# Full 128x128 tiles in place of four 128x32 column tiles, in stretches of TensorE work that hold no attention product

## The chip, the cores and the metric

The kernel runs on one core of one Trainium2 chip. The metric is the device time of one execution in microseconds. Before the change three runs gave 878.08, 880.55 and 883.79 us; the median is 880.55 us.

## The reference, cut to what matters

Two layers of one program, each an attention part A and an MLP part B, on 2048 tokens of width 576 in bf16:

```python
def _A_ref(x, wqkv, wo):          # 32 heads of 18, sliding window of 256, causal
    qkv = (x @ wqkv) ...
    scores = einsum("bhqd,bhkd->bhqk", q, k) * 18 ** -0.5
    p = softmax(where(mask, scores, -1e9))
    o = einsum("bhqk,bhkd->bhqd", p, v)
    return o.reshape(B, S, D) @ wo

def _B_ref(x, w1, b1, w2, b2):    # F = 4608
    h = gelu(layernorm(x) @ w1 + b1)
    return h @ w2 + b2

x = x + A(layernorm(x)); x = x + B(layernorm(x))   # both of these twice
```

The products with `w2` (the second MLP product) and with `wo` (the output product) are those that the change is about.

## The kernel before

Each layer is cut into four chunks of four token tiles (128 tokens each), eight chunks in all. For a chunk the kernel makes Q, K and V, the scores of eight groups of four heads, the exponentials, the product of the probabilities with V, the output product, layer norm, and the MLP in three parts of 12 blocks of 128 hidden columns. Work of neighbouring chunks is woven together, so that the exponentials of one chunk on ScalarE run while TensorE does the MLP of another.

Nothing of this order is written out by hand. Every step is a `Task` given to `Plan.add`, with its engine, its reads and writes, a cost and a priority. `Plan.schedule` simulates the engines and emits the tasks in the order of their simulated starts; a table of small nudges shifts priorities by stage. A task on TensorE has a `mode`, the tile shape in which it runs, and the planner adds `SWITCH` = 0.095 to the cost of a task whose mode differs from that of the task before:

- `"f"`: full 128x128 tiles. The QKV projection of chunk 0 (`two_out`, line 782), transposes, and the filler products (line 669).
- `"h"`: two tiles of 64 rows. The first MLP product (`G_part`, line 1058) and QKV of later chunks (line 822).
- `"r"`: four tiles of 32 rows, one for each head of a group. The scores (`scores`, line 891).
- `"c"`: four tiles of 32 columns. The product of probabilities with V (`pv`, line 938), which needs them since each head has only 20 columns, and all that goes through the helper `quad` (line 768): the second MLP product (`mm2`), the output product (`tail`, by `two_out`), and QKV of chunk 1 (also `two_out`).

`quad` computes what one full tile could: 128 rows, 128 output rows in PSUM, 288 moving columns. It issues four products of the same moving operand, each with 32 of the 128 stationary columns, into the four 32-partition parts of one bank. In this shape it can stand beside `pv` with no change of mode between them.

Each bank that a second MLP product fills collects 12 such quads, in two tasks of 6; one of the output product collects 5. VectorE then adds the bank to the residual (`resid`, lines 1001 to 1008). Scores are followed by exponentials on ScalarE (line 900) and the mask on GpSimd (line 921). Weights are loaded on SP's queue.

Of the kernel before, what the change touches and what calls it, by code (L numbers as in the profile page):

```python
# [158 lines left out]

class Task:  # L160
    __slots__ = ("idx", "eng", "fn", "reads", "writes", "cost", "lat", "prio", "dma", "ring", "handles", "alloc", "move", "desc",
                 "npred", "succ", "ready", "end", "plain", "fifo", "hold", "stage", "mode", "own", "port")

    def __init__(self, **kw):
        for k, v in kw.items():
# [21 lines left out]
class Plan:  # L187
# [18 lines left out]
        self.nudge = {}  # L206
        self.fifo_last = {}

    def add(self, eng, fn, reads=(), writes=(), dma=None, ring=4, cost=0.1, lat=0.1, prio=0.0, alloc=(), fifo=None, plain=False, after=(), move=0.0, desc=0, hold=False, mode="f", own=False, port=None):
        if eng == "dve" and fifo is None:  # L210
            fifo = self.chain
        stage = self.stage + self.part + ("+" if dma in ("w1", "w2", "xr") else "")
        prio += self.nudge.get(stage, 0.0)
        t = Task(idx=len(self.tasks), eng=eng, fn=fn, reads=tuple(reads), writes=tuple(writes), cost=cost, lat=lat, prio=prio,
                 dma=dma, ring=ring, alloc=tuple(alloc), handles=tuple({r for r in tuple(reads) + tuple(writes) if isinstance(r, Bank)}),
                 plain=plain, move=move, desc=desc, fifo=fifo, hold=hold, stage=stage, mode=mode, own=own,
                 port=(eng == "pool" and dma is None) if port is None else port)
        pred = set()
        for r in t.reads:
            if r in self.lw:  # L220
                pred.add(self.lw[r])
        for w in t.writes:
            pred.update(self.rd.get(w, ()))
            if w in self.lw:
                pred.add(self.lw[w])
        for w in after:
            pred.update(self.rd.get(w, ()))
        for w in t.writes:
            self.lw[w] = t
            self.rd[w] = []  # L230
        for r in t.reads:
            self.rd.setdefault(r, []).append(t)
        order = set()
        if fifo is not None:
            if fifo in self.fifo_last:
                order.add(self.fifo_last[fifo])
            self.fifo_last[fifo] = t
        order -= pred
        for p in pred:
            p.succ.append((t, True))  # L240
        for p in order:
            p.succ.append((t, False))
        t.npred = len(pred) + len(order)
        for h in t.handles:
            h.left += 1
        self.tasks.append(t)
        return t

    def keep_warm(self, a, b, bank_free, extra):

        if self.warm_fn is None or a < self.warm_from:
            a = max(a, self.warm_from)
        n = int((b - a - 0.1) * 0.8 / 0.115)
        banks = [x for x in (7, 6, 5, 4) if bank_free.get(x, 1e9) <= a]
        if n < 1 or not banks:
            return
        h = Bank(())
        h.no = banks[0]
        t = Task(idx=-1, eng="pe", fn=lambda e: self.warm_fn(e, h.no, n), reads=("warm",), writes=(h,), cost=n * 0.115, lat=0.1, prio=0.0,
                 dma=None, ring=4, alloc=(), handles=(), plain=False, move=0.0, desc=0, fifo=None, hold=False, stage="", mode="f", own=False, port=False)  # L260
        extra.append((a, t))

    def schedule(self):
        free = {e: BEGIN for e in ENGS}
        mode = "f"
        port = 0.0
# [49 lines left out]
        order = []  # L316
# [4 lines left out]
        while len(order) < n:  # L321
            best = None
            cands = []
            for e in ENGS:
                for t in released[e]:
                    st = max(free[e], t.ready)
                    if t.port:
                        st = max(st, port)
                    got = ()
                    if t.alloc:  # L330
# [3 lines left out]
                        st = max(st, when)  # L334
# [23 lines left out]
            if t.port:  # L358
                port = st + t.cost
# [5 lines left out]
            if t.dma is not None:  # L365
# [3 lines left out]
                while over > 0 and q:  # L369
                    a, b, d = q[0]  # L370
# [33 lines left out]
            order.append((st, t))  # L404
        order = sorted(order + extra, key=lambda x: x[0])
        self.order = order
        for st, t in order:
            names = lambda rs: [n for r in rs for n in ([f"pb{b}" for b in r.banks()] if isinstance(r, Bank) else [r])]
            if t.plain:
                self.S.plain(t.eng, t.fn)  # L410
            else:
                self.S.add(t.eng, t.fn, names(t.reads), names(t.writes), dma=t.dma, ring=t.ring, own=t.own)
# [11 lines left out]
def build_kernel(nc, A_x, A_wqkv, A_wo, B_x, B_w1, B_b1, B_w2, B_b2, out):  # L424
# [7 lines left out]
    KD = 5  # L432
    NF = F // P
    NPT = 3
    NFH = NF // NPT
# [3 lines left out]
    HB = 288  # L439
# [23 lines left out]
    add = PL.add  # L463
# [127 lines left out]
    def mm_cost(n):  # L591
        return max(n / 2400.0, 0.026) + (0.003 if n > 64 else 0.0)
# [69 lines left out]
    for i in OUT:  # L662
        b = Bank((i,))
# [89 lines left out]
    def w2_of(k, hf):  # L753
        return (w2_x, "w2x") if k == NK - 1 and hf == NPT - 1 else (w2_sb, "w2s")
# [7 lines left out]
                desc=128 * WB, prio=prio)  # L762


    def quad(e, b, lhs, rhs, start, stop):
        ins = None
        for j in range(4):
            ins = e.matmul(bank(b)[32 * j:32 * j + 32, 0:HB], lhs[:, 32 * j:32 * j + 32], rhs, start=start, stop=stop,  # L768
                           tile_position=(0, 32 * j), skip_group_check=True)
        return ins  # L770

    def two_out(lhs, rhs, reads, prio, after=(), fill=FILL, mode="f"):

        bs = [Bank(fill), Bank(fill)]
        for o in range(2):
            def fn(e, o=o):
                ins = None
                for c in range(KD):
                    if mode == "c":
                        ins = quad(e, bs[o], lhs(c), rhs(c, o * HB), c == 0, c == KD - 1)  # L780
                    else:
                        ins = e.matmul(bank(bs[o])[:, 0:HB], lhs(c), rhs(c, o * HB), start=(c == 0), stop=(c == KD - 1))  # L782
                return ins
            add("pe", fn, reads=reads, writes=[bs[o]], cost=mm_cost(HB) * KD, lat=0.22, prio=prio, alloc=[bs[o]], after=after, mode=mode)
        return bs

    def heads_of(b):
# [240 lines left out]
    def h_of(k, hf, fl):  # L1028
        if k == NK - 1 and hf == 1:
            return hP[:, fl, :], f"hp{fl}"  # L1030
        return hT[:, fl, :], f"h{fl}"
# [49 lines left out]
    def mm2(k, hf, prio):  # L1081
        l, t0, nt = CH[k]
        wt, wn = w2_of(k, hf)
        for i in range(nt):
            t = t0 + i
            fin = hf == NPT - 1 and l == NL - 1
            PL.part = f".{i}"
            osl, wait = None, []
            if fin and t >= 4:
                osl, odst, ord_ = f"x{t}", x_out[:, t - 4, :], [f"yo{t}h0", f"yo{t}h1"]  # L1090
            elif fin:
                sn = xn_ctr[0] % NXN
                xn_ctr[0] += 1
                osl, odst, ord_ = f"n{sn}", xn[:, sn, 0:D], [f"xn{sn}", f"xd{sn}"]
                wait = ord_
            for hh in range(2):
                b = Bank(FILL if k < NK - 1 else FILL + (3, 2, 1, 0))
                for f0 in range(0, NFH, 6):
                    def fn(e, hh=hh, b=b, f0=f0, i=i):
                        ins = None  # L1100
                        for fl in range(f0, f0 + 6):
                            ins = quad(e, b, h_of(k, hf, fl)[0][:, i * 128:(i + 1) * 128], wt[:, fl, hh * HB:(hh + 1) * HB],
                                       fl == 0, fl == NFH - 1)
                        return ins
                    add("pe", fn, reads=[h_of(k, hf, fl)[1] for fl in range(f0, f0 + 6 if f0 or i + hh == 0 or k == NK - 1 and i < 2 else NFH)] + [f"{wn}{f0 // WB}"], writes=[b],
                        cost=6 * mm_cost(HB), lat=0.22, prio=prio + 0.05 * i, alloc=((b,) if f0 == 0 else ()), mode="c",
                        after=(wait if f0 == 0 else ()))
                resid(t, hh, b, prio, outp=osl)
            if fin:
                dma("sp", out_dram[t * P:(t + 1) * P, :], odst, reads=ord_, cls="o", ring=4, cost=0.5,  # L1110
                    prio=prio)
            elif hf == NPT - 1:
                ln_stats(t, prio)
        PL.part = ""
# [28 lines left out]
    for i in range(n0):  # L1143
# [36 lines left out]
    for k in range(NK + 1):  # L1180
        b = 4 * k
# [114 lines left out]
```

## Time and profile before

| | |
|---|---|
| median of three runs | 880.55 us (878.08 to 883.79) |
| the profiled execution | 880.96 us, span 879.3 us |
| granted TensorE clock, mean | 0.994 |
| TensorE products (PE) | busy 856.9 us, 97% of the span, 17901 products |
| TensorE weight loads (PEld) | busy 543.0 us, 62% |
| ScalarE (ACT) | busy 594.7 us, 68% |
| VectorE (DVE) | busy 394.1 us, 45% |
| GpSimd (POOL) | busy 378.0 us, 43% |
| DMA | 120.58 MB, mean 137 GB/s |

How to read it: a row of the groups names a source line, an engine, an operation, the tile written and the tile read, the tile shape on the array as rows*columns (128*32 is a column tile, 128*128 a full one), the shapes, and a count; then busy time in us and mean duration in ns; then the idle time of the engine just before and what ended it. Busy time counts overlapping products once, so busy time by count is not the duration of one. A row of the timeline has start and length in us, the engine, the line, and how many instructions were merged. A row of the chain has start, length and what the chain went through.

### The profile page before, as it was taken

The numbers are of one execution on the slowest core, as the hardware profiler recorded it, in microseconds if no ns is written. First come the engines' busy times: TensorE is split into PE (matmuls) and PEld (weight loads), VectorE is DVE, ScalarE is ACT, GpSimd is POOL, SyncE is SP. The second block draws the span as 40 slices with busy tenths as digits, with TensorE's granted clock in tenths as the row PEclk, the third lists the DMA queues.
The fourth block names the chain that finished last, engine by engine and source line by source line (L and its number), as shares of the span: only waits on it lengthen the run. The fifth ranks groups of instructions, "written<-read, shape, count | busy, mean of one in ns | idle before, by whom it ended". The sixth has DMA issues, their size and how long they took to land.

```text
span 879.3 us, 39623 instructions
## 1 busy us (share of the span) xinstructions
PE 856.9 (97%) x17901; PEld 543.0 (62%) x17901; DVE 394.1 (45%) x934; ACT 594.7 (68%) x741; POOL 378.0 (43%) x560
## 2 busy tenths in 40 slices
PE   9888999999999999999999999999999899999998
PEld 7545556556566566565665665756656556557667
DVE  5877433555246442383434732654323353234012
ACT  4985797778667787564874887648687579771730
POOL 3875564385145662264431853426444176222100
PEclk9998999999999999999999999999999999999999
DMA  6799524471576722986367444675337963446320
GB/s 181 154 180 197 121 87 126 149 165 54 163 156 130 178 101 90 194 111 154 107 147 196 102 128 135 102 191 135 117 124 167 216 145 98 145 149 156 123 84 31
DMA packets 181913, 120.58 MB, mean 137 GB/s; under 512 B 107441, under 2 KB 181745, under 8 KB 181745
## 3 DMA queue, kind: packets, MB, share of 16 engines
q1 hardware_dynamic: 181744, 118.05, 55.1%
q8 instruction: 141, 2.31, 1.0%
q14 instruction: 28, 0.22, 0.1%
HBM read 90.10 MB, written 2.36 MB: 105 GB/s over the span
## 4 chain that ended last, share of the span: by engine, by line
PE 90%; DMA 5%; DVE 2%; issue 1%; ACT 1%; POOL 1%; SPq 0%; DVEq 0%; POOLq 0%
PE ps L768 36%; PE ps L1058 32%; PE ps L822 9%; PE ps L891 6%; PE ps L938 4%; DMA qT<-qn 2%; DMA xnTa<-xn 1%; DMA xnTm<-xn 1%; PE ps L782 1%; ACT pT L900 1%; PE ps L669 1%; DMA xnTm<-qn 1%; DMA kT<-qn 1%; POOL pT L921 0%; SPq L619 0%
## 5 line engine op out<-in xcount | busy, mean ns | idle before, releaser
L921 POOL TENSOR_SCALAR_AFFINE_SELECT pT<-pT 128x512 bf16<-128x512 bf16 (+1 forms) x368 | 282.6, 789 | 316.5 <-ACT pT L900 312.1
L900 ACT ACTIVATE pT<-ps 128x1024 bf16<-128x1024 f32 (+1 forms) x384 | 346.7, 971 | 82.3 <-PE ps L891 81.4
L768 PE MATMUL ps<-w_sb,hT 128*32 128x288 bf16 x8448 | 288.4, 287 | 1.9 <-issue 1.3
L1058 PE MATMUL ps<-xnTm,w_sb 64*128 64x512 bf16 x2592 | 288.3, 376 | 1.0 <-DVE st_all L682 0.4
L1068 ACT ACTIVATE hT<-ps,b1col 128x512 bf16<-128x512 f32 x276 | 167.4, 688 | 164.8 <-PE ps L1058 164.4
L768 PEld LDWEIGHTS ps<-w_sb,hT 128*32 128x32 bf16 x8448 | 216.8, 97 | 54.1 <-issue 21.3
L1058 PEld LDWEIGHTS ps<-xnTm,w_sb 64*128 64x128 bf16 x2592 | 128.7, 94 | 145.5 <-issue 6.4
L1001 DVE TENSOR_TENSOR x_res<-ps,x_res 128x288 f32<-128x288 f32 x224 | 100.5, 451 | 172.7 <-PE ps L768 172.1
L843 DVE CAST qn<-ps 128x288 bf16<-128x288 f32 x120 | 49.2, 451 | 145.8 <-PE ps L822 134.9
L822 PE MATMUL ps<-wqkv,xnTa 64*128 64x288 bf16 x1296 | 91.7, 286 | 1.8 <-DMA xnTa<-xn 1.4
L949 DVE STREAM_TRANSPOSE oq<-ps 128x512 f32<-128x512 f32 x64 | 45.7, 714 | 90.6 <-PE ps L938 90.1
L822 PEld LDWEIGHTS ps<-wqkv,xnTa 64*128 64x128 bf16 x1296 | 61.5, 95 | 30.9 <-issue 2.8
L891 PE MATMUL ps<-qT,kT 32*128 32x384 bf16 (+2 forms) x1216 | 64.7, 277 | 7.7 <-DMA qT<-qn 4.4
L1074 POOL TENSOR_TENSOR x_res<-x_res,b2bc 128x576 f32<-128x576 f32 x32 | 40.2, 1275 | 33.5 <-ACT hT L1068 33.4
L682 DVE BATCH_NORM_STATS2 st_all<-x_res 128x6 f32<-128x288 f32 (+1 forms) x128 | 53.7, 443 | 1.3 <-DMA x_res<-in_A_x_dram 0.4
L938 PE MATMUL ps<-pT,vA 128*20 128x384 bf16 (+2 forms) x1408 | 50.4, 276 | 1.6 <-DVE qn L843 1.4
L891 PEld LDWEIGHTS ps<-qT,kT 32*128 32x128 bf16 x1216 | 19.6, 92 | 48.4 <-issue 29.0
L768 PE MATMUL ps<-wo_sb,attT 128*32 128x288 bf16 x1280 | 44.0, 294 | 1.2 <-issue 1.2
L830 DVE CAST vA<-ps 128x288 bf16<-128x288 f32 x64 | 26.8, 451 | 39.6 <-PE ps L822 36.7
L768 PEld LDWEIGHTS ps<-wo_sb,attT 128*32 128x32 bf16 x1280 | 34.0, 99 | 10.4 <-issue 3.7
L707 DVE TENSOR_SCALAR xn<-x_res,mv_all,rstd 128x576 bf16<-128x576 f32 (+1 forms) x64 | 37.1, 593 | 7.2 <-DMA xnTm<-xn 6.1
L938 PEld LDWEIGHTS ps<-pT,vA 128*20 128x20 bf16 x1408 | 27.6, 91 | 19.2 <-issue 6.3
(52 smaller groups left out, 389.7 us busy)
## 6 DMA issues: line engine op xcount, KB each, us to landing
w_sb<-in_B_w_dram SPq DMA_DIRECT2D x46, 864.0 KB, 6.1
w_sb<-in_B_w_dram SPq DMA_DIRECT2D x48, 768.0 KB, 4.7
w_sb<-in_B_w_dram SPq DMA_DIRECT2D x96, 48.0 KB, 4.3
wqkv<-in_A_wqkv_dram SPq DMA_DIRECT2D x3, 576.0 KB, 5.5
x_res<-in_A_x_dram SPq DMA_DIRECT2D x3, 576.0 KB, 4.1
wqkv<-in_B_w_dram SPq DMA_DIRECT2D x2, 864.0 KB, 6.7
out_dram<-x_res SPq DMA_DIRECT2D x12, 144.0 KB, 2.0
wo_sb<-in_A_wo_dram SPq DMA_DIRECT2D x4, 144.0 KB, 3.5
```

What stands on the lines that cost most here:

```text
L682: add("dve", lambda e, i=i, s=s: e.bn_stats(st_all[:, t, i, :], s[:, t, i * HB:(i + 1) * HB]), reads=res, writes=[f"st{t}_{i}"], cost=0.37 ...
L768: ins = e.matmul(bank(b)[32 * j:32 * j + 32, 0:HB], lhs[:, 32 * j:32 * j + 32], rhs, start=start, stop=stop, tile_position=(0, 32 * j), sk ...
L822: ins = e.matmul(bank(bs[o])[:, 0:HB], xnTa[r:r + 64, c, i * 128:(i + 1) * 128], wqkv[r:r + 64, c, col:col + HB], start=(c == 4), stop=(ph ...
L843: add("dve", lambda e, b=bs[o], dst=dst: e.tensor_copy(dst, heads_of(bank(b))), reads=[bs[o]], writes=[f"qn{sl}h{o}"], cost=0.375, lat=0.1 ...
L891: ins = e.matmul(two(bs[j // 2])[:, j % 2, col:col + nq * 128], k_of(T0 + so)[0][32 * j:32 * j + 32, g, :], qs[32 * j:32 * j + 32, g, qo * ...
L900: add("act", lambda e, h2=h2: e.activation(pT[:, sl, 2 * h2:2 * h2 + 2, lo:hi], two(bs[h2])[:, :, lo:hi], ACT.Exp, scale=SCALE), reads=[bs ...
L921: add("pool", lambda e, ap=ap, pat=pat, sgn=sgn, kind=kind: e.affine_select(ap, ap, pattern=pat, compare_op=(ALU.is_ge if kind == "d" else ...
L938: ins = e.matmul(bank(bo)[32 * j:32 * j + VW, qo * 128:(qo + nq) * 128], vA[:, (T0 + so) % VS, 8 * j + g, :], pT[:, sl, j, col:col + nq * ...
L949: add("dve", lambda e: e.transpose(oq[:, 0:4 * nt, :].rearrange("p b c -> p (b c)"), bank(bo)[:, 0:nt * 128]), reads=[bo, f"aq{(g - 1) % G ...
L1001: add("dve", lambda e: e.tensor_tensor(x_res[:, t, sl], bank(b)[:, 0:HB], x_old[:, t, sl], ALU.add), reads=[b] + ([f"xin{t}"] if first els ...
L1058: ins = e.matmul(bank(bks[i])[:, 0:n], w1_sb[r:r + 64, sls[i], col:col + 128], xnTm[r:r + 64, k % 2, c, 0:n], start=(c == 4), stop=(ph == ...
L1068: add("act", lambda e, ff=ff, hd=hd, bk=bk: e.activation(hd[:, 0:n], bank(bk)[:, 0:n], ACT.Gelu_apprx_tanh, bias=b1col[:, ff:ff + 1]), rea ...
```

## The change

After the order has been settled, the planner walks over it once. It collects maximal stretches of consecutive TensorE tasks of mode `"c"`. Where every task of such a stretch goes through `quad` (it carries a list `wide`; `pv` has none), `wide` is set, and `quad` then emits one full 128x128 product instead of four column products. Costs, order, reads, writes and waits are untouched.

```diff
@@ Plan.schedule, behind the sorting of the order
         self.order = order
+        run = []
+        for st, t in order + [(0.0, None)]:
+            if t is not None and t.eng != "pe":
+                continue
+            if t is not None and t.mode == "c":
+                run.append(t)
+                continue
+            if all(x.wide is not None for x in run):
+                for x in run:
+                    x.wide[0] = True
+            run = []
         for st, t in order:
...
-    def quad(e, b, lhs, rhs, start, stop):
+    def quad(e, b, lhs, rhs, start, stop, wide):
+        if wide[0]:
+            return e.matmul(bank(b)[:, 0:HB], lhs, rhs, start=start, stop=stop, skip_group_check=True)
         ins = None
         for j in range(4):
             ins = e.matmul(bank(b)[32 * j:32 * j + 32, 0:HB], lhs[:, 32 * j:32 * j + 32], rhs, start=start, stop=stop,
...
@@ two_out
         for o in range(2):
-            def fn(e, o=o):
+            wide = [False]
+
+            def fn(e, o=o, wide=wide):
...
-                        ins = quad(e, bs[o], lhs(c), rhs(c, o * HB), c == 0, c == KD - 1)
+                        ins = quad(e, bs[o], lhs(c), rhs(c, o * HB), c == 0, c == KD - 1, wide)
...
@@ mm2
                 for f0 in range(0, NFH, 6):
-                    def fn(e, hh=hh, b=b, f0=f0, i=i):
+                    wide = [False]
+
+                    def fn(e, hh=hh, b=b, f0=f0, i=i, wide=wide):
...
                             ins = quad(e, b, h_of(k, hf, fl)[0][:, i * 128:(i + 1) * 128], wt[:, fl, hh * HB:(hh + 1) * HB],
-                                       fl == 0, fl == NFH - 1)
+                                       fl == 0, fl == NFH - 1, wide)
...
```

More of the change, by code (lines that the diff above doesn't have):

```diff
@@ L161 @@
     __slots__ = ("idx", "eng", "fn", "reads", "writes", "cost", "lat", "prio", "dma", "ring", "handles", "alloc", "move", "desc",
-                 "npred", "succ", "ready", "end", "plain", "fifo", "hold", "stage", "mode", "own", "port")
+                 "npred", "succ", "ready", "end", "plain", "fifo", "hold", "stage", "mode", "own", "port", "wide")
     def __init__(self, **kw):
@@ L207, in __init__, with add @@
         self.fifo_last = {}
-    def add(self, eng, fn, reads=(), writes=(), dma=None, ring=4, cost=0.1, lat=0.1, prio=0.0, alloc=(), fifo=None, plain=False, after=(), move=0.0, desc=0, hold=False, mode="f", own=False, port=None):
+    def add(self, eng, fn, reads=(), writes=(), dma=None, ring=4, cost=0.1, lat=0.1, prio=0.0, alloc=(), fifo=None, plain=False, after=(), move=0.0, desc=0, hold=False, mode="f", own=False, port=None, wide=None):
         if eng == "dve" and fifo is None:
@@ L216, in add @@
                  plain=plain, move=move, desc=desc, fifo=fifo, hold=hold, stage=stage, mode=mode, own=own,
-                 port=(eng == "pool" and dma is None) if port is None else port)
+                 port=(eng == "pool" and dma is None) if port is None else port, wide=wide)
         pred = set()
@@ L259, in keep_warm @@
         t = Task(idx=-1, eng="pe", fn=lambda e: self.warm_fn(e, h.no, n), reads=("warm",), writes=(h,), cost=n * 0.115, lat=0.1, prio=0.0,
-                 dma=None, ring=4, alloc=(), handles=(), plain=False, move=0.0, desc=0, fifo=None, hold=False, stage="", mode="f", own=False, port=False)
+                 dma=None, ring=4, alloc=(), handles=(), plain=False, move=0.0, desc=0, fifo=None, hold=False, stage="", mode="f", own=False, port=False, wide=None)
         extra.append((a, t))
@@ L783, in fn @@
                 return ins
-            add("pe", fn, reads=reads, writes=[bs[o]], cost=mm_cost(HB) * KD, lat=0.22, prio=prio, alloc=[bs[o]], after=after, mode=mode)
+            add("pe", fn, reads=reads, writes=[bs[o]], cost=mm_cost(HB) * KD, lat=0.22, prio=prio, alloc=[bs[o]], after=after, mode=mode, wide=wide)
         return bs
@@ L1102, in fn @@
                             ins = quad(e, b, h_of(k, hf, fl)[0][:, i * 128:(i + 1) * 128], wt[:, fl, hh * HB:(hh + 1) * HB],
-                                       fl == 0, fl == NFH - 1)
+                                       fl == 0, fl == NFH - 1, wide)
                         return ins
                     add("pe", fn, reads=[h_of(k, hf, fl)[1] for fl in range(f0, f0 + 6 if f0 or i + hh == 0 or k == NK - 1 and i < 2 else NFH)] + [f"{wn}{f0 // WB}"], writes=[b],
-                        cost=6 * mm_cost(HB), lat=0.22, prio=prio + 0.05 * i, alloc=((b,) if f0 == 0 else ()), mode="c",
+                        cost=6 * mm_cost(HB), lat=0.22, prio=prio + 0.05 * i, alloc=((b,) if f0 == 0 else ()), mode="c", wide=wide,
                         after=(wait if f0 == 0 else ()))
```

## Prediction

> **What bounds the kernel now.** I read the page first (busy shares, slices, chain), then TensorE's groups with shapes kept apart, then the list of waits, and last the timeline of TensorE where it changes from one tile shape to another.
>
> ```profile
> span 879.3 us, 39623 instructions
> ...
> PE 856.9 (97%) x17901; PEld 543.0 (62%) x17901; DVE 394.1 (45%) x934; ACT 594.7 (68%) x741; POOL 378.0 (43%) x560
> ...
> PEclk9998999999999999999999999999999999999999
> ...
> PE 90%; DMA 5%; DVE 2%; issue 1%; ACT 1%; POOL 1%; SPq 0%; DVEq 0%; POOLq 0%
> PE ps L768 36%; PE ps L1058 32%; PE ps L822 9%; PE ps L891 6%; PE ps L938 4%; DMA qT<-qn 2%; DMA xnTa<-xn 1%; DMA xnTm<-xn 1%; PE ps L782 1%; ACT pT L900 1%; PE ps L669 1%; DMA xnTm<-qn 1%; DMA kT<-qn 1%; POOL pT L921 0%; SPq L619 0%
> ```
>
> TensorE is busy 97% of the span at nearly full granted clock, and it is 90% of the chain that ended last. L768, the line of the column-tile helper `quad`, alone is 36% of that chain. So a nanosecond saved or lost on a TensorE product counts nearly in full, and no other engine can hide it. The groups say what the changed line is made of.
>
> ```profile
> L768 PE MATMUL ps<-w_sb,hT 128*32 128x288 bf16 x8448 | 288.4, 287 | 1.9 <-issue 1.3 <-DVE x_res L1001 0.5
> L768 PE MATMUL ps<-wo_sb,attT 128*32 128x288 bf16 x1280 | 44.0, 294 | 1.2 <-issue 1.2
> L768 PE MATMUL ps<-wqkv,xnTa 128*32 128x288 bf16 x480 | 18.1, 288 | 1.0 <-issue 0.8 <-DVE qn L843 0.2
> L782 PE MATMUL ps<-wqkv,xnTa 128*128 128x288 bf16 x120 | 16.9, 286 | 0.3 <-issue 0.3
> L768 PE MATMUL ps<-w_sb,pT 128*32 128x288 bf16 x384 | 12.3, 286 | 0.0
> L768 PE MATMUL ps<-wqkv,hT 128*32 128x288 bf16 x384 | 12.3, 286 | 0.0
> ```
>
> The L768 rows together hold 8448 + 1280 + 480 + 384 + 384 = 10976 products, 2744 quads of four. Row L782 is what the change puts in their place: 120 full 128x128 products with the same 288 moving columns, in the projections of the first chunk. A quad and a full product do the same arithmetic; the duration of one (286 ns) tells nothing, since products overlap. What counts is the distance from one start to the next.
>
> **The change part by part.** The order of instructions after the change is the same on all five engines, and so are the waits: no step moves, no DMA moves, and nothing is added on the queues of SP and POOL. Of the 2744 quads 1948 become one full product each, in 112 stretches: 1578 of 2304 second-MLP quads, 280 of 320 of the output projection, and 90 of 120 of the second chunk's QKV projection, which goes through the same helper. 69 of the stretches are 12 quads long. 106 of the 112 come after a score product (row tiles) and 104 have one behind them; the rest stand beside 64-row tiles or at the end. The 796 quads in stretches with an attention product keep their tiles. 3 x 1948 = 5844 products and as many weight loads go, of 17901 each. A stretch pays for three things: its pitch, the way in and the way out.
>
> Pitch. First a run of full products and then two of quads.
>
> ```profile
> 16.57 3.23 PE L782 MATMUL ps<-wqkv,xnTa 128*128 128x288 bf16 x25
> 19.63 0.61 PE L856 MATMUL ps<-ident,qn 128*128 128x128 bf16 x8
> ...
> 563.29 3.86 PE L768 MATMUL ps<-w_sb,hT 128*32 128x288 bf16 x120
> 566.98 0.83 PE L938 MATMUL ps<-pT,vA 128*20 128x384 bf16 x24
> ...
> 829.12 11.87 PE ps L768 x384
> 840.99 11.76 PE ps L1058 x108
> 852.75 23.66 PE ps L768 x768
> 876.41 0.03 issue
> ```
>
> 25 full products took 19.63 - 16.57 = 3.06 us to the next full-size instruction, 122.4 ns each. 30 quads took 566.98 - 563.29 = 3.69 us to an attention product in the same tile shape, 123.0 ns, of which the first quad after a shape change holds some 10 ns more. The 96 quads at 829.12 took 11.87 us with one shape change behind them; less 0.11 for that (below) it is 122.5 ns each. So the four column products truly run side by side, and the pitch is the same. Between the ends: 0.5 ns either way x 1948 = 1.0 us either way. I take 0.
>
> The way in. Score product to the first product behind it, once to a full product and twice to a quad, with the same 384-column scores ahead:
>
> ```profile
> 21.48 0.34 PE L891 MATMUL ps<-qT,kT 32*128 32x384 bf16 x4
> 21.75 2.01 PE L782 MATMUL ps<-wqkv,xnTa 128*128 128x288 bf16 x15
> 23.82 0.34 PE L891 MATMUL ps<-qT,kT 32*128 32x384 bf16 x4
> 24.09 0.42 PE L782 MATMUL ps<-wqkv,xnTa 128*128 128x288 bf16 x2
> ...
> 379.78 0.34 PE L891 MATMUL ps<-qT,kT 32*128 32x384 bf16 x4 [0.24 <-DMA qT<-qn]
> 380.05 2.39 PE L768 MATMUL ps<-w_sb,hT 128*32 128x288 bf16 x72
> 382.37 0.34 PE L891 MATMUL ps<-qT,kT 32*128 32x256 bf16 x8
> ...
> 451.70 0.34 PE L891 MATMUL ps<-qT,kT 32*128 32x384 bf16 x4
> 451.97 0.31 PE L768 MATMUL ps<-w_sb,hT 128*32 128x288 bf16 x4
> ```
>
> It is 0.27 us in all four, 0.16 of it the streaming of 384 columns at the pitch above and 0.11 the change of shape. Rounding leaves 0.01 us either way, x 112 = 1.1 us. I take 0.
>
> The Trainium skill, TensorEngine Tiling, section "Restrictions and Gotchas", says that column tiling excludes Fast Weight Load, so the weight loads on the way in should get quicker; TensorE: Matmul & The Clock Gate, section "Weight-path perf modes", has that mode measured at about twice the speed. By that rule I would estimate half of a 97 ns load, 0.05 us, x 112 = 5 us gained. The trace does not agree: 97 and 98 ns in its rows for the two kinds of load, and the same 0.27 us, so I give it nothing.
>
> ```profile
> L768 PEld LDWEIGHTS ps<-w_sb,hT 128*32 128x32 bf16 x8448 | 216.8, 97 | 54.1 <-issue 21.3 <-ACT hT L1068 1.1 <-DVE x_res L1001 1.0
> ...
> L782 PEld LDWEIGHTS ps<-wqkv,xnTa 128*128 128x128 bf16 x120 | 10.9, 98 | 3.9 <-issue 1.2 <-DVE qn L843 0.2 <-DVE st_all L682 0.2
> ```
>
> The way out. From the quads at 380.05 it is 382.37 - 380.05 - 18 x 0.1225 = 0.115 us over their streaming. Full products have few clean ways out in this trace. The clearest rows:
>
> ```profile
> 21.14 0.38 PE L669 MATMUL ps<-warm 128*128 128x256 bf16 x2
> ...
> 60.93 0.39 PE L669 MATMUL ps<-warm 128*128 128x256 bf16 x2
> 61.26 0.42 PE L822 MATMUL ps<-wqkv,xnTa 64*128 64x288 bf16 x4
> ```
>
> Two fillers of 256 columns stream for 2 x 122.5 x 256/288 = 218 ns. The way from there to 64-row tiles is 61.26 - 60.93 - 0.218 = 0.11 us, and to the scores at 21.48 it is 0.12 us. So out of a full product costs what it costs out of a quad, within 0.01 us. One small gain is left: the four products of a quad start one after another, and the shape can change only once the last one is through. The single quad at 451.97 lasts 0.31 us and one product 0.287, so its last start is at most 0.02 us behind its first. A full product has no such tail. I take 0.01 us, between 0 and 0.02: 112 x 0.01 = 1.1 us gained, between 0 and 2.2.
>
> No edit is costed at nothing for being off the path but one: the load of the next weights lies under the 122 ns product before it (98 ns). Uncovered, it is the third rival below.
>
> The sum goes against the profiled execution, 880.96 us with a span of 879.3 us (1.7 us lie around it): 880.96 + 0 + 0 - 1.1 = 879.9 us. That execution is 0.4 us over the median of 880.55 us, and the three runs reach from 878.08 to 883.79, so the forecast gain is smaller than their spread. A measurement of this kernel can tell about 1%, 8.8 us, from no change.
>
> **The rivals.** First, a gain at the sequencer.
>
> ```profile
> PEld ps L891 <- issue: 35.6, 134, 2.0
> ...
> PE ps L768 <- issue: 3.3, 6, 0.9
> ...
> PE ps L891 <- issue: 2.3, 2, 1.8
> ```
>
> TensorE's products at L768 and L891 stand idle for 5.6 us with nothing to wait for that the profile shows. With 11688 instructions fewer the sequencer could run further ahead, and this could vanish: 879.9 - 5.6 = 874.3 us, still within 1%. For it speaks that a quad is eight instructions in 122 ns; against it, that one of the longest gaps is in an output projection that shares its stretch with attention products and keeps its tiles:
>
> ```profile
> 576.47 0.80 PE L768 MATMUL ps<-wo_sb,attT 128*32 128x288 bf16 x20 [0.70 <-issue]
> ```
>
> Second, on the other side: the way out of a full tile into the 32-row score tiles is dearer than out of column tiles. One mechanism, at the 104 places where scores follow. For it: the 15 full products at 21.75 reach the scores at 23.82 at 23.82 - 21.75 - 15 x 0.1225 = 0.23 us over their streaming, 0.12 us more than quads; x 104 = 12.5 us, 880.96 + 12.5 = 893.5 us, 1.4% slower. It decides from 8.8/104 = 0.085 us on. Against it, those scores waited for ScalarE to empty their banks, which went on to 23.76, and the way at 21.14, where the scores do not wait that long, is 0.12 us:
>
> ```profile
> 22.24 1.52 ACT L900 ACTIVATE pT<-ps 128x768 bf16<-128x768 f32 x2
> ```
>
> Third, also slower: the next weights of a full tile cannot be loaded while the product before runs, since both use all 128 rows and columns; each of the 1948 would then show its 98 ns, 191 us, and the time would be 880.96 + 191 = 1072 us. The 122.4 ns pitch of the 25 full products above speaks against it: it leaves no room for a 98 ns load. The Trainium skill, TensorE: Matmul & The Clock Gate, section "Part 3: Packing small matmuls", has this rule: weight loads overlap running products only where their row groups differ. The trace does not agree; quads and full products alike use all rows, and both keep a pitch of about 122 ns.
>
> Fourth, a large gain: a change of shape to or from full tiles is cheaper than measured here. Each stretch pays about 0.11 + 0.115 us for both, 112 x 0.225 = 25.2 us, and if half of it went the time would be 880.96 - 12.6 = 868.4 us, 1.4% faster. It decides from 8.8/112 = 0.079 us a stretch. Nothing above speaks for it: 0.27 us in and 0.11 out are the same for full tiles. That the change does not do what it says is no rival with a time of its own: the built kernel holds the 1948 full products. What could disappoint is that a long stretch has nothing to gain, such as the 192 quads at 852.75, which end the kernel.
>
> **How the numbers follow.** My forecast, 879.9 us, has a chance of 0.70; the gain at the sequencer 0.14; the dearer way out 0.08; exposed weight loads 0.01; the cheaper change of shape 0.07. The first two lie within 1%, so: same 0.84, slower 0.08 + 0.01 = 0.09, faster 0.07. The bounds of the sum are pitch 1.0, way in 1.1 and way out 1.1 either side of its value; all together 879.9 + 3.2 = 883.1 and 879.9 - 3.2 = 876.7. The range goes down to the sequencer's 874.3 and up to 886.0, 883.1 with the 2.8 us that the highest of the three runs lies over the profiled one. With the first two cases inside it and the edges of the others it leaves some 2 in 10 out.
>
> **What would show it right or wrong.** In the profile after: full products at a pitch of 122.5 ns and quads at the same; scores still 0.27 us ahead of the first product behind them; the way from full products to scores about 0.105 us over their streaming; TensorE's busy time about 1 us less with 12057 products; weight loads much less busy, at no gain. The issue waits at L768 and L891 tell the first rival. A pitch near 220 ns would prove the third, a way out above 0.2 us the second, and a way in under 0.2 us the fourth. I am wrong if the time leaves 874.3 to 886.0 us without a bank or a transfer being waited for.

## The result, and the profile after

The change made the kernel faster: 871.31 us, median of 6 runs (869.34 to 875.01), against 880.92 us for the kernel before beside it (878.08 to 889.35). The ratio is 0.9885, with a 95% interval from 0.9837 to 0.9933. The forecast was 879.9 us with a range from 874.3 to 886.0; the time lies 3.0 us under the range, and the gain of 9.6 us is about nine times the 1.1 us forecast.

The profiled execution after took 869.34 us. From its page: the span, the engines, the granted clock, the instruction queue, and the chain that ended last.

```profile
span 867.6 us, 27935 instructions
...
PE 849.3 (98%) x12057; PEld 521.6 (60%) x12057; DVE 393.5 (45%) x934; ACT 593.6 (68%) x741; POOL 377.5 (44%) x560
...
PEclk9999999999999999999999999999999999999999
...
q8 instruction: 95, 1.56, 0.7%
...
PE 92%; DMA 4%; DVE 1%; issue 1%; SPq 1%; ACT 0%; POOL 0%; DVEq 0%; POOLq 0%
PE ps L1073 32%; PE ps L778 27%; PE ps L781 11%; PE ps L837 9%; PE ps L906 6%; PE ps L953 5%; PE ps L797 2%; DMA qT<-qn 1%; SPq L630 1%; DMA xnTm<-qn 1%; PE ps L680 1%; DMA x_res<-in_A_x_dram 1%; DMA xnTm<-xn 1%; DMA kT<-qn 1%; DVE qn L858 1%
```

The products are the 12057 that were to be left, TensorE is still the bound, and its share of the chain rises from 90% to 92%. Lines have moved by 10 to 15: the full tiles stand at L778, the quads that are left at L781, the scores at L906. The row "q8 instruction" is the one that the prediction passed over. It counts the packets (and their MB) by which TensorE's own instructions are brought in. The same row of the kernel before:

```profile
q8 instruction: 141, 2.31, 1.0%
```

The trace of before holds 36110 TensorE instructions (weight loads, products, waits), the trace of after 24422. Divided by 141 and 95 packets that is 256 and 257: a packet of 16.4 KB brings 256 instructions. It is a small transfer, 1% of the DMA engines' time. What matters is when each packet comes.

TensorE's groups of after, with shapes kept apart (last column: idle time before them, and what ended it), and its list of waits:

```profile
L778 PE MATMUL ps<-w_sb,hT 128*128 128x288 bf16 x1386 | 185.9, 287 | 0.0
...
L781 PE MATMUL ps<-w_sb,hT 128*32 128x288 bf16 x2904 | 99.8, 286 | 0.2 <-DVE xn L1023 0.2
```

```profile
PE ps L906 <- DMA qT<-qn: 3.7, 2, 2.5
...
PE ps L797 <- issue: 0.3, 1, 0.3
```

Before, the same second-MLP row at L768 had 1.3 us of "issue", the output projection 1.2, QKV 0.8, and the waits named 3.3 us at L768 and 2.3 at L891. After, only the 0.3 us at L797, the first chunk's full tiles, is left; before had it too. The 5.6 us of the first rival no longer stand in the list.

**Where the 11.7 us between the two spans lie.** I took each trace's products in order of start and set off the time in which a product's columns stream. That is 0.416 ns a column at full clock: products of 288 columns follow each other at 122.5 ns, products of 72 columns (in the kernel of four pieces below) at 32.6 ns, so 216 columns more take 89.9 ns. Then I sorted what is left of each distance from one start to the next: up to 16 ns as pitch, up to 120 ns as change of shape, and the rest by whether TensorE had a wait for a semaphore in it, or the clock was granted at half.

```
us                                         before   after
columns streaming                           782.5   782.5
rest of the pitch                            18.1    17.5
412 changes of shape                         43.9    42.9
gaps with no wait                             5.3     0.0
waits on semaphores                          16.4    15.2
streaming at half clock                       3.9     0.2
first 31 us, and from the last product on     9.2     9.3
sum                                         879.3   867.6
```

What the prediction priced, pitch and shapes, moved by 1.6 us. The other 10 us are dead time, and half of that lies in gaps with no wait.

**What a gap with no wait is.** The timeline of TensorE at one of them, first before and then after at the same place in the order:

```profile
139.54 1.40 PE L768 MATMUL ps<-w_sb,hT 128*32 128x288 bf16 x37
141.80 0.55 PE L768 MATMUL ps<-w_sb,hT 128*32 128x288 bf16 x11 [0.86 <-issue]
142.28 0.40 PE L891 MATMUL ps<-x_res,kT 32*128 32x256 bf16 x8
```

```profile
134.42 1.64 PE L778 MATMUL ps<-w_sb,hT 128*128 128x288 bf16 x12
136.00 0.40 PE L906 MATMUL ps<-x_res,kT 32*128 32x256 bf16 x8
```

Before, the 12 quads stop after 37 of their 48 products: in the middle of a quad, where nothing is to be waited for. I numbered TensorE's instructions in the trace in order of start, and set beside each such gap above 0.2 us the fetch packet that landed last ahead of it:

```
before: work resumes  gap     at instruction number    fetch packet     resumes after it landed
          57.18 us   0.93 us   1729 = 256 *   6 + 193    54.70- 55.73    1.45 us
          81.06      0.32      2497 = 256 *   9 + 193    78.72- 79.65    1.41
         141.80      1.03      4801 = 256 *  18 + 193   139.34-140.36    1.44
         273.78      0.54     10433 = 256 *  40 + 193   271.12-272.18    1.60
         576.47      0.87     23489 = 256 *  91 + 193   574.18-575.11    1.36
         734.67      0.63     29889 = 256 * 116 + 193   732.29-733.41    1.26
         765.12      0.68     31169 = 256 * 121 + 193   762.76-763.83    1.29
         794.63      0.25     32449 = 256 * 126 + 193   792.25-793.33    1.31
after:   none
```

All eight begin at the same place of a block of 256, and end 1.3 to 1.6 us after a packet landed. TensorE had run out of instructions. At 65 instructions a microsecond (a quad is eight in 122.5 ns) a block lasts 3.9 us. The fetch before the gap at 141.80 started 2.71 us after TensorE had passed the block boundary at 136.63, took 1.02 us, and its first instruction ran 1.44 us later: 5.17 us in all, more than the block could cover. A full tile is two instructions in 122.5 ns, so a block of them lasts 15.7 us. After the change some fetches start even later (up to 4.7 us behind the boundary), and TensorE waits for none. What the change takes away is blocks that are used up fast: with the stalls left out, 66 of the 140 blocks of before lasted under 4.5 us, and 6 of the 94 after. From the boundary to the landing a fetch took about as long in both, 1.8 and 1.7 us in the median.

The longest gap that the list of before puts down to "issue", 1.8 us at 66.91, is not among the eight. The weight load behind it waits for a semaphore, for which the view names nobody, and it is instruction 2034, at no block boundary. So of the 5.6 us of the first rival some 3.8 belong to the shortage.

### The profile page after: what moved, and what is told of

Its sections match the earlier page's. It is cut to its first block, busy times and chain, and to the rows that moved or that the text cites. A ratio compares the mean times of both kernels' runs of the same rounds, so it can differ in the third digit from the quotient of the medians.

```text
span 867.6 us, 27935 instructions
## 1 busy us (share of the span) xinstructions
PE 849.3 (98%) x12057; PEld 521.6 (60%) x12057; DVE 393.5 (45%) x934; ACT 593.6 (68%) x741; POOL 377.5 (44%) x560
## 4 chain that ended last, share of the span: by engine, by line
PE 92%; DMA 4%; DVE 1%; issue 1%; SPq 1%; ACT 0%; POOL 0%; DVEq 0%; POOLq 0%
PE ps L1073 32%; PE ps L778 27%; PE ps L781 11%; PE ps L837 9%; PE ps L906 6%; PE ps L953 5%; PE ps L797 2%; DMA qT<-qn 1%; SPq L630 1%; DMA xnTm<-qn 1%; PE ps L680 1%; DMA x_res<-in_A_x_dram 1%; DMA xnTm<-xn 1%; DMA kT<-qn 1%; DVE qn L858 1%
## 5 line engine op out<-in xcount | busy, mean ns | idle before, releaser
L778 PE MATMUL ps<-w_sb,hT 128*128 128x288 bf16 x1386 | 185.9, 287 | 0.0
L778 PEld LDWEIGHTS ps<-w_sb,hT 128*128 128x128 bf16 x1386 | 128.3, 98 | 48.5 <-issue 15.0
L781 PE MATMUL ps<-w_sb,hT 128*32 128x288 bf16 x2904 | 99.8, 286 | 0.2 <-DVE xn L1023 0.2
L781 PEld LDWEIGHTS ps<-w_sb,hT 128*32 128x32 bf16 x2904 | 75.2, 97 | 14.7 <-issue 3.1
L906 PE MATMUL ps<-qT,kT 32*128 32x384 bf16 (+2 forms) x1216 | 64.2, 277 | 8.1 <-DMA qT<-qn 3.7
L906 PEld LDWEIGHTS ps<-qT,kT 32*128 32x128 bf16 x1216 | 19.5, 92 | 48.5 <-issue 28.7
```

Source lines behind the costliest of these rows:

```text
L778: return e.matmul(bank(b)[:, 0:HB], lhs, rhs, start=start, stop=stop, skip_group_check=True)
L906: ins = e.matmul(two(bs[j // 2])[:, j % 2, col:col + nq * 128], k_of(T0 + so)[0][32 * j:32 * j + 32, g, :], qs[32 * j:32 * j + 32, g, qo * ...
```

## The experiments

Three theories stood against each other. Supply: TensorE ran out of instructions, and fewer of them are what helps. Tile: the full tile itself is quicker than was measured, in a change of shape or in its stream. Clock: the granted clock is higher after the change (0.998 for 0.994 in the profiled executions). The first four experiments ran on one chip with 29 runs of the kernel before (median 880.67 us), the other three on another (29 runs, median 881.99). Dead time and gaps come from one trace of each kernel.

**The kernel before once more**, to see which gaps belong to the program and which to the run. No edit.

> The kernel before, unchanged, for a second profile and the granted clock of each of its runs. Theory 1 (TensorE runs out of instructions): its profile again has gaps on TensorE with nothing named that they wait for, 4 to 6 us in all, most of them in the same places as in the first profile. Theory 2 (every way into or out of a full tile is cheaper): says nothing here. Theory 3 (the granted clock): the runs spread by their clock; where it is 0.998 the kernel before takes some 877 us, where it is 0.994 some 881 us, and the median of all stays at 879 to 882 us.

Measured: 880.15 us (875.71 to 885.1, 12 runs), ratio 0.9996 (0.9968 to 1.0024). Its timeline at the place shown above:

```profile
136.37 1.40 PE L768 MATMUL ps<-w_sb,hT 128*32 128x288 bf16 x37
138.08 0.55 PE L768 MATMUL ps<-w_sb,hT 128*32 128x288 bf16 x11 [0.32 <-issue]
```

The gap stands behind the same 37th product, at instruction 4801, but it is 0.48 us and not 1.03. Six of the eight gaps come again at the same instruction numbers; together they take 2.5 us where they took 5.3, and not the 4 to 6 us expected. Place belongs to the program, size to the run. The span was the same all the same (879.2 us), since waits on semaphores took 21.4 us in place of 16.4. An engine that is late for one reason may wait less for the next; two traces do not prove it. Gaps, waits and half clock together are 25.5 us here and 25.6 in the first trace. So it is this sum that is compared below, as dead time.

**Two 64-column tiles in place of one full tile**, in the same 112 stretches: half the instructions go, instead of three quarters, and the shape is still a column tiling.

```diff
         if wide[0]:
-            return e.matmul(bank(b)[:, 0:HB], lhs, rhs, start=start, stop=stop, skip_group_check=True)
+            for j in range(2):
+                ins = e.matmul(bank(b)[64 * j:64 * j + 64, 0:HB], lhs[:, 64 * j:64 * j + 64], rhs, start=start,
+                               stop=stop, tile_position=(0, 64 * j), skip_group_check=True)
+            return ins
```

> In the same 112 stretches two column tiles of 64 in place of four of 32: 4 instructions for 122 ns of work where before has 8 and the full tile 2. Theory 1: 32 instructions per us can be delivered as well as 16, the gaps go, and the time is within 1.5 us of the full tile's, 870 to 873 us. Theory 2: half of what the full tile brings, about 876 us. Theory 3: nothing but the clock, 879 to 882 us at the clock of before.

Measured: 872.03 us (868.2 to 874.8, 6 runs), ratio 0.9898 (0.9856 to 0.994). That is nearly all of the gain with no full tile in any of these stretches. Dead time is 16.2 us. One gap above 0.2 us is left, in a stretch that keeps its quads, and the wait behind it shows what such a gap may hide:

```profile
688.73 0.43 PE L784 MATMUL ps<-w_sb,hT 128*32 128x288 bf16 x7 [1.11 <-issue]
689.61 0.40 PE L909 MATMUL ps<-qT,kT 32*128 32x384 bf16 x8 [0.45 <-DMA qT<-qn]
```

So most of the gain needs no full tile; half the instructions fewer are enough for it.

**Full tiles with the old number of instructions**: each product of 288 columns is cut into four of 72.

```diff
         if wide[0]:
-            return e.matmul(bank(b)[:, 0:HB], lhs, rhs, start=start, stop=stop, skip_group_check=True)
+            for j in range(4):
+                ins = e.matmul(bank(b)[:, 72 * j:72 * j + 72], lhs, rhs[:, 72 * j:72 * j + 72],
+                               start=start and j == 0, stop=stop and j == 3, skip_group_check=True)
+            return ins
```

> Full 128x128 tiles in the 112 stretches as in the change, but each product of 288 columns cut into four of 72, so that TensorE again gets 8 instructions for one product. The pitch of four pieces becomes 130 to 135 ns by the 2.5 ns that each product costs above its columns: 1948 x 7.5 to 12.5 ns = 15 to 24 us on top. Theory 1: gaps with no named wait come back, 2 to 6 us in all, and the time is 888 to 900 us. Theory 2: no such gaps, 884 to 894 us.

Measured: 890.36 us (885.7 to 893.32, 10 runs), ratio 1.01 (1.0067 to 1.0132): slower than the kernel before. The cut costs 14.1 us of pitch by its trace (32.1 us against 18.1, some 7 ns for each of the 1948), which is no part of the question. The gaps are back, at the instruction numbers 1729, 2497, 4801, 10433, 23489, 29889 and 31169 of the kernel before, with one of 1.4 us at a new one, 28353, and 8.0 us together, more than the 2 to 6 expected:

```profile
138.81 0.75 PE L779 MATMUL ps<-w_sb,hT 128*128 128x72 bf16 x18
140.12 0.52 PE L779 MATMUL ps<-w_sb,hT 128*128 128x72 bf16 x11 [0.56 <-issue]
...
578.76 0.79 PE L783 MATMUL ps<-wo_sb,attT 128*32 128x288 bf16 x20
582.18 0.80 PE L783 MATMUL ps<-wo_sb,attT 128*32 128x288 bf16 x20 [2.63 <-issue]
```

The second pair is the output projection of the first rival (576.47 us before, again 2.79 us here at number 23489). A full tile with eight instructions runs dry where a quad with eight does. Dead time in its trace is 24.6 us, as before the change. That execution, at 893.32 us, was the longest of the ten, though: the median less the 14.1 us is 876.3 us, so by the medians some 4 us of the gain may have stayed with the full tile, at the old number of instructions. (The median itself lies in the ranges of both theories; the gaps tell them apart, not the time.) A piece of four lasts 130 ns where a quad lasts 122.5, so a block of 256 lasts some 0.2 us longer; whether this is the reason was not tried.

**The kernel before with its block boundaries shifted**: twice as many filler products of half the length near the start, 80 instructions more and no other edit.

```diff
-        for _ in range(n):
-            ins = e.matmul(bank(bk)[:, 0:256], warm[:, :], warm[:, :].unsqueeze(1).to_broadcast([P, 2, P]), start=True, stop=True)
+        for _ in range(2 * n):
+            ins = e.matmul(bank(bk)[:, 0:128], warm[:, :], warm[:, :], start=True, stop=True)
```

> The kernel before with its filler products at the start cut into two of half the columns each: 40 products and 40 weight loads more, nearly all in the first 9 us and in the same time, so that every later instruction stands some 70 places further back in the stream, a quarter of the 256 that one 16 KB fetch holds. Theory 1: the gaps without a named wait are 3 to 8 us again, but at other places, and the time is 877 to 885 us. Theories 2 and 3: nothing changes, and gaps that belong to the program's own places stay where they are.

Measured: 881.2 us (877.58 to 886.9, 12 runs), ratio 1.0017 (0.9986 to 1.0049). None of the old eight places has a gap. There are four others of the kind, of 0.20 to 0.77 us and 1.5 us together (3 to 8 were expected), again at 256k + 193 each, among them one in the middle of a stretch that ran through before:

```profile
519.25 0.92 PE L768 MATMUL ps<-w_sb,hT 128*32 128x288 bf16 x24
520.78 0.92 PE L768 MATMUL ps<-w_sb,hT 128*32 128x288 bf16 x24 [0.61 <-issue]
```

This tells supply from any cause that sits in the work itself: the work is the same, the gaps moved with the numbering. That the time stayed the same speaks against winning anything by placing the boundaries, as far as one shift can.

**The change in the short stretches alone** (12 quads or fewer: 84 stretches, 946 quads) **and in the long ones alone** (28 stretches, 1002 quads). A cause per stretch would put three quarters of the gain on the short ones; a cause per instruction would halve it.

```diff
-            if all(x.wide is not None for x in run):
+            quads = sum(round((x.cost - (SWITCH if x is run[0] else 0.0)) / 0.123) for x in run)
+            if all(x.wide is not None for x in run) and quads <= 12:     # in the other kernel: quads > 12
```

> The change only in stretches of at most 12 quads: 84 of the 112 stretches, 946 of the 1948 quads. Theory 1 (TensorE runs out of instructions): the gain lies where instructions fall short, and with 49% of the dense instructions gone about half of the 9 us comes, time 874 to 878 us; some gaps without a named wait stay, in the stretches that keep their quads. Theory 2 (every way into or out of a full tile is cheaper): 84/112 of the gain, 873 to 874 us, no matter how long the stretches are.

> The change only in stretches of more than 12 quads: 28 of the 112 stretches, 1002 of the 1948 quads, 420 of them in the last 75 us, where nothing was short. Theory 1: about half of the 9 us, 873 to 878 us; gaps without a named wait are 0 to 3 us. Theory 2: 28/112 of the gain, 878 to 879 us.

Measured: 876.91 us for the short ones (874.28 to 879.89, 12 runs; ratio 0.9941, 0.9916 to 0.9966), 876.84 for the long ones (872.26 to 884.76, 12 runs; ratio 0.9961, 0.9929 to 0.9994). By the medians that is 5.1 and 5.2 us of gain: halves, as the quads are, and together about the gain of the whole. The intervals are wide, though: from 3.0 to 7.4 us and from 0.5 to 6.3 us, so three quarters on the short ones (7.2 us) and one quarter on the long ones (2.4 us) are not ruled out by them. At equal granted clock the long ones bring more, not less: the short ones gain 5.0 us at 0.996 (3 runs), 3.4 at 0.998 (5) and 3.3 at 1.000 (4), the long ones 6.9 at 0.996 (6) and 7.4 at 0.998 (3). That speaks against a cause per stretch, and leaves the even halves in doubt. Dead time is 23.0 and 22.7 us, and blocks used up in under 4.5 us are 30 and 38. Both still run dry, and where they do, it is at quads, or at the work next to them (first row pair: short ones, second: long ones):

```profile
656.73 0.78 PE L782 MATMUL ps<-w_sb,hT 128*32 128x288 bf16 x19
658.81 0.79 PE L782 MATMUL ps<-w_sb,hT 128*32 128x288 bf16 x17 [1.30 <-issue]
```

```profile
595.59 0.39 PE L907 MATMUL ps<-qT,kT 32*128 32x256 bf16 x5
597.93 0.29 PE L907 MATMUL ps<-qT,kT 32*128 32x256 bf16 x3 [1.95 <-issue]
```

**Fewer instructions still**: on top of the change, two 64-column tiles for each quad that stands beside attention products.

```diff
-        for j in range(4):
-            ins = e.matmul(bank(b)[32 * j:32 * j + 32, 0:HB], lhs[:, 32 * j:32 * j + 32], rhs, start=start, stop=stop,
-                           tile_position=(0, 32 * j), skip_group_check=True)
+        for j in range(2):
+            ins = e.matmul(bank(b)[64 * j:64 * j + 64, 0:HB], lhs[:, 64 * j:64 * j + 64], rhs, start=start, stop=stop,
+                           tile_position=(0, 64 * j), skip_group_check=True)
```

> The change, and in the stretches that hold attention products each quad is two column tiles of 64 beside the attention products' column tiles of 32, in place of four of 32: 3184 instructions fewer, and 67 places where a tile of 64 columns stands next to one of 32. If such a change of width costs what a change from row to column tiles costs (0.11 us): 67 x 0.11 = 7.4 us, time 876 to 880 us. If it costs nothing: the time of the change, or up to 1 us less, 869 to 872 us, since theory 1 sees no gap left to close.

Measured: 874.35 us (870.62 to 879.11, 10 runs), ratio 0.9926 (0.9902 to 0.9951): no better than the change alone, and between the two ranges expected. Dead time falls again, to 13.3 us, but there are 479 changes of shape for 412, and they take 49.6 us for 42.9: 6.7 us for 67 more, 0.10 us each. From 64 columns to the 32 of the attention product is such a change; first this kernel, then the one before at the same place, where there is none:

```profile
283.66 0.93 PE L781 MATMUL ps<-w_sb,hT 128*64 128x288 bf16 x12
284.51 0.83 PE L953 MATMUL ps<-pT,vA 128*20 128x384 bf16 x24
285.27 0.93 PE L781 MATMUL ps<-w_sb,hT 128*64 128x288 bf16 x12
```

```profile
287.93 0.92 PE L768 MATMUL ps<-w_sb,hT 128*32 128x288 bf16 x24
288.68 0.83 PE L938 MATMUL ps<-pT,vA 128*20 128x384 bf16 x24
289.33 0.91 PE L768 MATMUL ps<-w_sb,hT 128*32 128x288 bf16 x24
```

Six quads to the attention product: 0.85 us against 0.75. The attention product to the next quad: 0.76 against 0.65.

**All kernels side by side**, instruction packets from the page of each, dead time from one trace each:

```
                      packets   dead time, us   of it gaps / waits / half clock   median against before
before                  141        25.6            5.3 / 16.4 / 3.9
before again            141        25.5            2.5 / 21.4 / 1.5                 -0.5 us
before, shifted         141        25.4            1.5 / 20.8 / 3.1                 +0.5
four pieces             141        24.6            8.0 / 13.7 / 2.9                 +9.7 (14.1 of it pitch)
short stretches         119        23.0            2.2 / 19.4 / 1.4                 -5.1
long stretches          117        22.7            1.7 / 18.0 / 3.0                 -5.2
two 64-column tiles     110        16.2            2.7 / 13.5 / 0.0                 -8.6
after                    95        15.4            0.0 / 15.2 / 0.2                 -9.6
two tiles beside too     83        13.3            0.7 / 12.7 / 0.0                 -7.6 (6.7 lost in shapes)
```

(A gap at a boundary that also holds a wait counts as a wait here; the shifted kernel has two such, of 2.27 and 1.47 us, and the long stretches two, of 2.11 and 1.43 us. Told by instruction number alone, the gaps are 5.2 us for the long stretches, 1.4 for two 64-column tiles and none for two tiles beside too.) The sum of dead time falls with the number of instructions brought in. How much of that the tile itself does is not settled: the trace of four pieces has the full tile and the dead time of before, but its median leaves room for some 4 us.

**The clock.** Every run has its granted clock beside its time. The kernel before and its repeat on the first chip took, by the median, 884.24 us at 0.994 (9 runs), 880.7 at 0.996 (13), 879.24 at 0.998 (14) and 876.08 at 1.000 (3): the clock makes much of the spread from run to run. The kernel after took 875.01 us at 0.994 (1 run), 873.66 at 0.996 (2) and 870.23 at 0.998 (3), on a chip that its runs do not name; two 64-column tiles, on the first chip, 872.8 at 0.998 (2) and 870.55 at 1.000 (3). So 5.5 to 6.4 us of gain stay at equal clock on one chip, and 7 to 9 in the comparison across chips, which is rougher: on the second chip the kernel before took 880.64 us at 0.998 (12) and 879.21 at 1.000 (5), 1.4 and 3.1 us more than on the first. Stretches at half clock, of 3.4 or 6.8 us, are part of the dead time. Behind the first 31 us and ahead of the end the nine traces show ten, and each begins during a stall of 1.3 us or more or within 1.8 us of its end; that of 583.42 us in the four pieces follows the 2.8 us at number 23489. Not every such stall has one: after the change one of 2.6 us at 688.63 has none. So a part of the half clock comes with the stalls, and need not be a cause of its own.

**What stays open.** That the gaps without a wait are a shortage of instructions is shown: by their numbers, by the shift, and by the four pieces. They are 2.5 to 5.3 us of some 10. The rest is fewer and shorter waits, about half of them for transposing DMAs (7.3 us of the list of waits before, 6.5 after), and less half clock. By the traces its size falls with the number of instructions too, but why is not settled, and the median of the four pieces does not bear it out. A pointer is the time from issue to landing of two kinds of transpose, before and then after:

```profile
xnTm<-xn SPq DMA_TRANSPOSE x32, 3.0
...
kT<-qn SPq DMA_TRANSPOSE x26, 4.3
```

```profile
xnTm<-xn SPq DMA_TRANSPOSE x32, 2.6
...
kT<-qn SPq DMA_TRANSPOSE x26, 3.4
```

They land 0.4 and 0.9 us sooner; the other two large kinds hardly do (qT 4.2 and 4.1 us, xnTa 3.8 and 3.7). Whether the packets of instructions stand in their way, or a TensorE that stalls less simply spreads them better, no experiment here tells.

## Why the prediction was wrong, point by point

- **Pitch, 0: right.** 48 full products at 846.91 us of the trace after took 5.88 us to the next, 122.5 ns each, with the weight loads hidden. This ends the third rival.

```profile
846.91 6.04 PE L778 MATMUL ps<-w_sb,pT 128*128 128x288 bf16 x48
852.79 3.10 PE L778 MATMUL ps<-wqkv,hT 128*128 128x288 bf16 x24
```

- **Way in and way out, -1.1 us: right.** The 412 changes of shape took 43.86 us before and 42.90 after, 0.96 us less. In steady alternation (first before, then after) score follows score at 1.913 us before (5.74 us for three) and 1.907 after (5.72 for three):

```profile
309.72 0.40 PE L891 MATMUL ps<-qT,kT 32*128 32x384 bf16 x8
310.05 1.65 PE L768 MATMUL ps<-w_sb,hT 128*32 128x288 bf16 x48
...
315.46 0.40 PE L891 MATMUL ps<-qT,kT 32*128 32x384 bf16 x8
```

```profile
304.12 0.40 PE L906 MATMUL ps<-qT,kT 32*128 32x384 bf16 x8
304.45 1.64 PE L778 MATMUL ps<-w_sb,hT 128*128 128x288 bf16 x12
...
309.84 0.40 PE L906 MATMUL ps<-qT,kT 32*128 32x384 bf16 x8
```

  The way in is still 0.33 us behind eight scores and the way out is no dearer, so the second and the fourth rival are out too.

- **The step that failed is the first rival, the gain at the sequencer.** The forecast put the term at nothing and gave it a chance of 0.14. As far as the gaps go it was the right mechanism. The argument against it was the row at 576.47 us, an output projection that keeps its tiles. That row was read as if the cause had to sit in the tiles beside the gap. It sits in the instruction number: 23489 is the first of a fetched block, and the block before it is used up at 65 instructions a microsecond. After the change that projection, still in quads, runs through:

```profile
562.76 5.08 PE L781 MATMUL ps<-wo_sb,attT 128*32 128x288 bf16 x160
```

  A boundary lies in it here too, at 565.58 us, but at another place, and the fetch began 1.36 us behind the boundary before it, where it had been 2.55; the packet landed 1.64 us ahead. So at this one place the gap went with the timing of the fetch, and that is luck as far as the record shows. Over the whole kernel it went with the number of fast blocks, 66 to 6. A count of the instructions up to each named gap, and the queue row of 141 packets, would have turned this argument round; both were in the trace of before.

- **Its price was too low.** It was set to the 5.6 us of named "issue" waits, as the most that could go, and 1.8 of these were no such gap. The two traces show 10.2 us of dead time less, of which the gaps with no wait are half or less. The prediction took the list of waits as fixed but for the rows named "issue"; the second trace of the kernel before shows that gaps and waits can shift against each other (5.3 and 16.4 us, 2.5 and 21.4) at the same sum.

- **The lower end of the range, 874.3 us, fell with that price.** The statement that the kernel's last 192 quads gain nothing held: they stream at 122.5 ns before and after. Two slips in the working change nothing: 883.1 and 2.8 make 885.9, and two of the four ways in, not one, lead to a full product.

## What to carry to other kernels

A busy engine can be short of instructions: divide 256 instructions by the rate at which a stretch uses them, and compare with the time that a fetch takes from the block boundary (here 2.3 to 2.7 us once it starts, until the first instruction runs, and 1.9 to 3.5 us until it does, at the gaps of before). Where two ways of tiling have the same pitch, the one with fewer instructions is the safer one. To name a gap without a wait, number the engine's instructions and see whether the gaps stand at a fixed remainder; one extra trace of the same program tells what of a wait belongs to the program.

## What the runs showed of the hardware that was not expected

- TensorE's instructions come in packets of 256, and a late packet stops it for 0.2 to 2.8 us. The Trainium skill, Runtime: NRT & Kernel Launch, section "Instruction fetch mechanics", has the 16 KiB blocks of 256, and this trace agrees (2.31 MB in 141 packets); it also says that the cost of passing a boundary is mostly hidden, which held at all boundaries after the change and failed at 8 of the 140 of before, where quads and the work next to them use up 256 instructions in 4.0 to 5.5 us.
- The first instruction of a block runs 1.2 to 1.6 us after its packet has landed, in all 8 gaps of before and all 6 of the same kernel again; at the gap of two 64-column tiles it was 2.3 us.
- Between 64-column and 32-column tiles a change of shape costs 0.10 us (67 more took 6.7 us), like the others in this kernel (412 took 43.9).
- Half clock set in, in all ten cases between the first 31 us and the end, during a stall of 1.3 us or more or within 1.8 us of its end.
- A full product of 288 columns cut into four of 72 costs some 7 ns more, 14.1 us over 1948.
